# Feed-forward and projections in four 128-row column tiles instead of eight 64-row tiles, beside attention that stays in 64-row tiles

## The chip, the cores and the metric

One core of a Trainium2 chip runs the kernel. The metric is device time in microseconds (us); the median of two runs before the change is 1071.32 us (1070.79 to 1071.85). A change of 2% is 21.4 us.

The core has a matrix engine (TensorE, in the profile PE, with its weight loads as PEld), a vector engine (DVE), a scalar engine (ACT), a general engine (POOL) and queues that issue transfers (SP above all). Matmul results go to PSUM, a memory of 128 partitions that DVE and ACT read.

## The reference

```python
x = A_x                                            # 1 x 2048 x 512, float32
g = _sigmoid((x * gate_w).sum(-1, keepdims=True))
# attention: 32 query heads of 16 columns, one shared key and value head
q = (x @ wq).reshape(B, S, H, Dh).transpose(0, 2, 1, 3); k = x @ wk; v = x @ wv
p = softmax(einsum("bhqd,bkd->bhqk", q, k) * Dh ** -0.5)
a = einsum("bhqk,bkd->bhqd", p, v) ... reshape(B, S, H * Dh) @ wo
b = silu(x @ w1) @ w2                              # 512 -> 1792 -> 512
return g * a + (1 - g) * b
```

## The kernel before

All operands of the large products are split into two float16 parts, and a product of two such operands is three matmuls (high by high, high by low, low by high). The product of low by low is left out.

**Prologue** (`first_pass`, up to about 34 us): x comes in by transfers of 256 rows (`loads`, L305), is transposed on PE (`transposed`, L317) and split into `xs`; keys and values are made (`K`, L387), and the first two blocks of queries (`Q`, L125 to L127).

**Attention and feed-forward** (`attention`, the rest) are interleaved by hand on PE. There are 512 steps: 4 chunks of 512 queries, 4 groups of heads, 2 halves of a group, 16 tiles of 128 keys. The loop at L1082 takes two steps at a time; call one trip a *pair*. There are 256 pairs. A pair's order of work on PE is a string with one letter for each piece:

- `S` (`scores`, L1012): eight matmuls of 50 rows (contraction) by 32 columns, one for each of two row halves and four column strips of the array, 512 long. ACT then takes the exponential of 128 x 1024 (L1015). Four `S` a pair.
- `P` and `N` (`pv`, L1058): eight matmuls of 64 rows by 32 columns. A step is either one float32 product (`N`) or three short ones (`P`): upper half of the probabilities by `VH` and by `VL`, and the rest of them, which DVE has computed (`low`, L1036), by `VH`.
- `F`: one *slot* of the stream of other products: feed-forward up (`ffn_h`) and down (`ffn_o`), query blocks (`q_block`) and output projection (`out_proj`). Six slots a pair, in two *bursts* of three, and twelve (two bursts of six) where the pair is widened.

The two usual strings are `SFFFSFFFSPPPSBN` and `SFFFSFFFSNBSN`; the widened ones have `FFFFFF` for `FFF`. The first pair has its own, with `E` for products on the whole 128 by 128 array (`whole`, L766).

An output of the stream is a 128 x 512 block in one PSUM bank (`pM`, two banks). It has 12 products of 128 rows (6 in the last feed-forward group), and each goes to the array as matmuls of 32 columns (`Out.product`, L762). The stream (`stream`) works on two outputs at a time. In a slot a product of the *new* output goes to the upper 64 rows of the array (`lo`, four column strips) and a product of the *current* output to the lower 64 rows (`hi_`). So an output is visited twice, once for each half of the contraction, and its evacuation (`evict`) comes after the second visit. `drain` is called between the two visits at the very end alone (`ending`).

Late in the run (at 778 us), `gather` (L643) collects the largest values that were met, writes 128 numbers to DRAM (`md`, L649), reads them back as a row (L654) and sets a flag, by which a second pass of the whole would run with other scales. It does not run here.

Of the kernel before, what the change touches and what calls it, by code (L numbers as in the profile page):

```python
# [6 lines left out]
F32 = mybir.dt.float32  # L7
# [38 lines left out]
def kernel(  # L46
# [21 lines left out]
    nc = tc.nc  # L68
    _, S, D = x.shape
    F = w1.shape[1]  # L70
    DH = wk.shape[1]
    KD = D // 128
# [4 lines left out]
    x = x.rearrange("b s d -> (b s) d")  # L77
# [16 lines left out]
    ident = consts.tile([128, 128], F32)  # L94
# [110 lines left out]
    def identity(cst):  # L205
        jp = cst.tile([128, 128], F32)
        nc.gpsimd.iota(jp, pattern=[[1, 128]], base=0, channel_multiplier=-1, allow_small_or_imprecise_dtypes=True)
        nc.vector.tensor_scalar(ident, jp, 0.0, None, op0=OP.is_equal)
# [81 lines left out]
    def loads(sb, q_cols):  # L290

        wkr = sb.tile([128, KD, DH], F32)
        nc.scalar.dma_start(wkr, by_row(wk))
        wvr = sb.tile([128, KD, DH], F32)
        nc.scalar.dma_start(wvr, by_row(wv))
        gwr = sb.tile([128, KD], F32)
        nc.scalar.dma_start(gwr, gate_w.rearrange("(p k) -> p k", k=KD))
        xn = []
        wqr = sb.tile([128, KD, q_cols], F32)
        for c in range(NCH):  # L300
            t_ = sb.tile([128, 4, D], F32, name=f"xn{c}")
            if c == NCH - 1:
                nc.sync.dma_start(wqr, by_row(wq)[:, :, :q_cols])
            for a in range(2):
                nc.sync.dma_start(t_[:, 2 * a:2 * a + 2], x[c * 512 + a * 256:c * 512 + a * 256 + 256].rearrange("(t p) d -> p t d", p=128))  # L305
            xn.append(t_)
        wkv = sb.tile([128, KD, 64], F32)
        nc.gpsimd.memset(wkv, 0.0)
        nc.gpsimd.tensor_copy(wkv[:, :, 0:16], wkr)
        nc.gpsimd.tensor_copy(wkv[:, :, 32:48], wvr)  # L310
        nc.gpsimd.tensor_copy(flat(wkv[:, :, 48:49]), gwr)
        return xn, wqr, wkv
# [44 lines left out]
    def first_pass():  # L357
        with ExitStack() as pro:
            sb = pro.enter_context(tc.tile_pool(name="pro", bufs=1))
            wk_ = pro.enter_context(tc.tile_pool(name="prow", bufs=2))  # L360
            ps = pro.enter_context(tc.tile_pool(name="props", bufs=1, space=PSUM))
            identity(sb)
            nc.gpsimd.memset(mxs, 0.0)
            sel_k, selA, selB, m_one, hmask, m_k = masks(sb)
            xn, wqr, wkv = loads(sb, 256)
# [262 lines left out]
    def chores():  # L628

        todo = []  # L630
        for kt in range(KD):
            for h in range(2):
                todo.append(lambda kt=kt, h=h: absmax(mxs[:, M_X + 2 * kt + h:M_X + 2 * kt + h + 1], xs[:, 0, kt, h * S // 2:(h + 1) * S // 2]))
                todo.append(lambda kt=kt, h=h: absmax(mxs[:, M_1 + 2 * kt + h:M_1 + 2 * kt + h + 1], w1s[:, 0, kt, h * F // 2:(h + 1) * F // 2]))
        for f in range(0, FT_ALL, 2):
            todo.append(lambda f=f: absmax(mxs[:, M_2 + f // 2:M_2 + f // 2 + 1], flat(w2s[:, 0, f:f + 2])))
        for o in range(0, NO, 2):
            todo.append(lambda o=o: absmax(mxs[:, M_O + o // 2:M_O + o // 2 + 1], flat(wo_s[:, 0, o:o + 2])))

        todo.append(lambda: absmax(mxs[:, M_Q:M_Q + 1], flat(wqs[:, 0])))  # L640
        todo.append(lambda: absmax(mxs[:, M_VV:M_VV + 1], VF[:, :, 0:16], AX.XY))

        def gather():  # L643
            mt, mr = raw_[0][:, 0:32], raw_[0][:, 32:33]
            nc.vector.tensor_reduce(mr[0:64], um, axis=AX.X, op=OP.min)
            nc.vector.tensor_scalar(mxs[0:64, M_B:M_B + 1], mr[0:64], -1.0, SHIFT * LAM / ONE, op0=OP.mult, op1=OP.add)
            nc.vector.transpose(mt, mxs)
            nc.vector.tensor_reduce(mr, mt, axis=AX.X, op=OP.max)
            nc.sync.dma_start(md.rearrange("(p o) -> p o", o=1), mr)  # L649

        m, m1 = raw_[1][0:1, 0:128], raw_[1][0:1, 128:160]

        def row():
            nc.sync.dma_start(m, md.rearrange("(o p) -> o p", o=1))  # L654

        g = raw_[2][0:1, 0:4 * len(RANGES)].rearrange("p (a b) -> p a b", a=4)

        def check(n0):
            if n0 == 0:
                nc.vector.tensor_reduce(m1, m.rearrange("p (a b) -> p b a", a=4), axis=AX.X, op=OP.max)  # L660
            for n in range(n0, min(n0 + 3, len(RANGES))):
                a, b, lo, hi = RANGES[n]
                nc.vector.tensor_reduce(g[:, 0, n:n + 1], m1[:, a:b], axis=AX.X, op=OP.max)
                nc.vector.tensor_scalar(g[:, 1, n:n + 1], g[:, 0, n:n + 1], lo, None, op0=OP.is_lt)
                nc.vector.tensor_scalar(g[:, 2, n:n + 1], g[:, 0, n:n + 1], hi, None, op0=OP.is_gt)

        def verdict():
            nc.vector.tensor_tensor(g[:, 3], g[:, 1], g[:, 2], op=OP.max)
            nc.vector.tensor_reduce(g[:, 0, 0:1], g[:, 3], axis=AX.X, op=OP.max)
            nc.vector.tensor_copy(flag, g[:, 0, 0:1])  # L670

        return todo, gather, row, *(lambda n=n: check(n) for n in range(0, len(RANGES), 3)), verdict


# [47 lines left out]
    def attention(ctx, scale_of, t_scale, shifts, split_pieces, chores, q_todo, bounds, early, gates_):  # L722
# [187 lines left out]
            return o  # L910

        seq, ahead, ended, debt = outs(), [], [None], [18]
        drains, left = [0], [4 * len(blocks)]
        turn = [None, 0]
        lo, hi_ = slice(0, 64), slice(64, 128)
        plain, ending = [False], [False]

        def stream():

            cur = None  # L920
            while True:
                if plain[0] and cur is None:
                    return
                new = None if plain[0] else follow()
                n_new = len(new.mm) if new else 0
                n_cur = len(cur.mm) if cur else 0
                n = -(-max(n_new, n_cur) // 6) * 6


                if cur and drains[0] == cur.count and ending[0]:  # L930
                    drain()
                for i in range(n):
                    turn[:] = cur, n - i - 1
                    for m in range(4):
                        if i < n_new:
                            new.product(i, lo, m, i == 0, False)
                        if i < n_cur:
                            cur.product(i, hi_, m, False, i == n_cur - 1)
                    if i < n - 1:
                        yield False  # L940
                if cur:
                    cur.evict(cur.bank)
                    ended[0] = cur
                cur = new
                if cur:
                    cur.count = drains[0]
                yield True

        def drain():

            nc.tensor.drain()
            drains[0] += 1

        def norm_a(pv, rb, st):

# [125 lines left out]
        prefetch(0)  # L1081
        for s in range(0, len(steps) + 2, 2):  # L1082
            on = s < len(steps)
            ending[0] = not on
            if on and steps[s][1] == 0:
                i = steps[s][0]
                prefetch(i + 1)
                if q_todo and i % 2 == 0:
                    queue.append(q_todo.pop(0))
            p, more = 2 * s, True  # L1090
            slots, order = SPLIT, [(s - 2, 0), (s - 2, 1), (s - 2, 2), (s - 1, 3)]
            if s - 2 in native:
                slots, order = NATIVE, [(s - 2, 3), (s - 1, 3)]
            if not s and early:
                slots = FIRST
            wide[0] = debt[0] >= 6 and ended[0] is not None and ended[0].hidden
            if wide[0]:
                slots = WIDE[slots]
            ended[0], n_f, bounded[0] = None, 0, False
            for a in slots:  # L1100
                if a == "S" and on:
                    scores(p)
                    p += 1
                elif a == "E":
                    next(whole_, None)
                elif a == "F" and more:
                    more = not next(work)
                    n_f += 1
                elif a == "B" and (bound_now() or s == 4 and bounds):
                    bound()  # L1110
                    bounded[0] = True
                    while lq and lq[0][0] <= p - 3:
                        low(*lq.pop(0))
                elif a in "PN" and s >= 2:
                    pv(*order.pop(0))
            debt[0] -= max(n_f - 6, 0)
            if gates_ and s == 4:
                gates_()
                spend(0.6)
            fill(4.95 if n_f > 6 else 4.1 if ended[0] and ended[0].hidden else 3.7)  # L1120
# [65 lines left out]
```

## Time and profile before

| what | value |
|---|---|
| median of the runs | 1071.32 us |
| the profiled execution | 1071.37 us, its span 1069.5 us |
| granted TensorE clock | 0.998 |
| PE busy | 1047.9 us, 31236 matmuls |
| PEld busy | 662.3 us, 31236 weight loads |
| ACT busy | 1006.2 us, 1116 instructions |
| DVE busy | 769.8 us, 1064 instructions |
| POOL busy | 24.2 us, 54 instructions |

The span is from the first to the last instruction. Busy time is the union of an engine's instructions; matmuls overlap one another, so the start of one and the start of the next tell more than a duration does. A shape such as 64*32 in the profile is the rows by columns of the array that a matmul uses.

### The profile page before, as it was taken

Reading aid. Unit: us, or ns where it says so; the run is one execution under the profiler, and the core shown is the slowest. Engines: PE = TensorE matmul, PEld = TensorE weight load, DVE = VectorE, ACT = ScalarE, POOL = GpSimd, SP = SyncE. Lnnn points to the kernel's source line nnn. Section 1 sums busy time; section 2 is a strip of 40 time slices with the busy share of each in tenths; the row PEclk is TensorE's granted clock in tenths of the full one; section 3 lists DMA queues with packets and bytes.
Section 4 is the critical chain, followed back from the end, with each engine's and each line's share of the span. In section 5 each row is a group of like instructions: output and inputs, shape, how many; then the busy total and the mean of one; then the engine's idle time right before and its main releaser. Section 6 shows DMA issues by size and latency. Waiting matters only on the chain.

```text
span 1069.5 us, 65974 instructions
## 1 busy us (share of the span) xinstructions
PE 1047.9 (98%) x31236; PEld 662.3 (62%) x31236; DVE 769.8 (72%) x1064; ACT 1006.2 (94%) x1116; POOL 24.2 (2%) x54
## 2 busy tenths in 40 slices
PE   7999999999999999999999999999999999999996
PEld 5456766667566577766655567686756565555552
DVE  6676776677778686978776696775857767475875
ACT  5899999999999999999999999899989999999993
POOL 1110010100000000000000000000000000000000
PEclk9999999999999999999999999999999999999999
DMA  6321111210001000000000100000000010000001
GB/s 219 108 66 43 44 47 45 61 41 21 6 11 50 22 22 12 14 12 21 12 11 21 39 27 12 22 12 12 22 4 11 31 32 12 12 7 8 12 4 44
DMA packets 20840, 32.95 MB, mean 31 GB/s; under 512 B 5137, under 2 KB 12050, under 8 KB 20562
## 3 DMA queue, kind: packets, MB, share of 16 engines
q1 hardware_dynamic: 17618, 20.46, 6.0%
q0 software_dynamic: 2512, 8.13, 2.6%
q8 instruction: 246, 4.03, 1.6%
q14 instruction: 32, 0.26, 0.1%
q10 hardware_dynamic: 432, 0.07, 0.0%
HBM read 20.12 MB, written 8.52 MB: 27 GB/s over the span
## 4 chain that ended last, share of the span: by engine, by line
PE 90%; ACT 4%; DVE 3%; issue 2%; DMA 1%; SPq 0%; POOL 0%; DVEq 0%; POOLq 0%; ACTq 0%
PE pv L1058 36%; PE pm L762 32%; PE S L1012 20%; ACT P L1015 4%; PE pt L317 1%; DVE acc L743 0%; DMA xn<-in_A_x_dram 0%; DVE T L958 0%; PE pk L387 0%; DVE U L959 0%; DMA raw<-in_B_w_dram 0%; DVE T L960 0%; DVE C L965 0%; DMA qd<-qs__367 0%; DMA qb<-qd 0%
## 5 line engine op out<-in xcount | busy, mean ns | idle before, releaser
L1015 ACT ACTIVATE P<-S 128x1024 f32<-128x1024 f32 x1024 | 964.0, 1050 | 24.7 <-PE S L1012 15.9
L1012 PE MATMUL S<-qb,KT 50*32 50x512 f16 x8192 | 478.1, 378 | 2.7 <-issue 1.4
L1036 DVE TENSOR_TENSOR L<-P 128x1024 f16<-128x1024 f32 x332 | 389.4, 1217 | 7.1 <-ACT P L1015 7.1
L1058 PE MATMUL pv<-P,VF 64*32 64x512 f32 x5536 | 383.1, 589 | 0.4 <-issue 0.4
L1012 PEld LDWEIGHTS <-KT 50*32 50x32 f16 x8192 | 188.8, 90 | 193.7 <-issue 124.7
L762 PE MATMUL pm<-w2s,H 64*32 64x512 f16 x5328 | 261.4, 375 | 0.6 <-issue 0.2
L762 PE MATMUL pm<-xs,w1s 64*32 64x512 f16 x5376 | 249.3, 375 | 1.3 <-DVE acc L743 0.6
L762 PEld LDWEIGHTS <-H 64*32 64x32 f16 x5328 | 144.6, 93 | 45.8 <-issue 12.7
L762 PEld LDWEIGHTS <-w1s 64*32 64x32 f16 x5376 | 136.2, 93 | 43.8 <-issue 12.5
L1058 PEld LDWEIGHTS pv<-P,VF 64*32 64x32 f32 x5536 | 127.4, 107 | 32.1 <-issue 10.1
L811 DVE SCALAR_TENSOR_TENSOR e<-e,pm 128x512 f32<-128x512 f32 x56 | 38.4, 686 | 141.4 <-ACT e L810 141.3
L762 PE MATMUL pm<-xs,wqs 64*32 64x512 f16 x1152 | 79.7, 375 | 0.0
L1058 PE MATMUL pv<-P,VH 64*32 64x512 bf16 x1328 | 77.6, 389 | 0.0
L1058 PE MATMUL pv<-P,VL 64*32 64x512 bf16 x1328 | 77.2, 385 | 0.0
L1058 PE MATMUL pv<-L,VH 64*32 64x512 f16 x1328 | 76.2, 374 | 0.0
L1058 PEld LDWEIGHTS <-VH 64*32 64x32 f16 x2656 | 56.9, 92 | 18.2 <-issue 2.3
L762 PE MATMUL pm<-wo_s,O 64*32 64x512 f16 x1440 | 64.3, 375 | 0.0
L743 DVE SCALAR_TENSOR_TENSOR acc<-pm,g,acc 128x512 f32<-128x512 f32 x47 | 35.0, 745 | 31.5 <-PE pm L762 31.5
L958 DVE STREAM_TRANSPOSE T<-pv 128x512 f32<-128x512 f32 x32 | 22.9, 717 | 48.1 <-PE pv L1058 36.9
L762 PEld LDWEIGHTS <-wqs 64*32 64x32 f16 x1152 | 41.8, 93 | 11.7 <-issue 3.6
L762 PEld LDWEIGHTS <-O 64*32 64x32 f16 x1440 | 30.0, 93 | 17.2 <-issue 2.6
L810 ACT ACTIVATE e<-pm 128x512 f32<-128x512 f32 x56 | 34.4, 615 | 6.4 <-PE pm L762 6.4
(159 smaller groups left out, 463.4 us busy)
## 6 DMA issues: line engine op xcount, KB each, us to landing
qb<-qd SPq DMA_DIRECT2D x192, 32.0 KB
raw<-in_B_w_dram POOLq DMA_DIRECT2D x23, 256.0 KB, 3.1
xn<-in_A_x_dram SPq DMA_DIRECT2D x8, 512.0 KB
out_dram<-acc SPq DMA_DIRECT2D x16, 256.0 KB
qd<-qx SPq DMA_DIRECT2D x12, 256.0 KB
raw<-in_A_wo_dram POOLq DMA_DIRECT2D x4, 256.0 KB, 2.9
qb<-sh SPq DMA_DIRECT2D x62, 2.0 KB
raw<-in_B_w_dram SPq DMA_DIRECT2D x3, 256.0 KB
```

Of the source, the lines that this page charges most:

```text
L317: nc.tensor.transpose(pt[:, kt], xn[c].rearrange("p t (d k) -> p t k d", k=KD)[:, t, kt], ident)
L743: nc.vector.scalar_tensor_tensor(a, po, gate[:, n:n + 1], a, op0=OP.mult, op1=OP.add)
L762: nc.tensor.matmul(self.bank[32 * m:32 * m + 32], l(i, rows, 32 * m), r(j, rows), start=first, stop=last)
L810: nc.scalar.activation(e, ph, AF.Tanh, scale=t_scale)
L811: nc.vector.scalar_tensor_tensor(e, e, 1.0, ph, op0=OP.add, op1=OP.mult)
L958: nc.vector.transpose(T, pv[0])
L1012: nc.tensor.matmul(sc[32 * m:32 * m + 32, f], KT[b:b + 50, k0:k0 + 32], qtile[i][b:b + 50, j], start=True, stop=True)
L1015: nc.scalar.activation(P[:, 2 * j:2 * j + 2], sc, AF.Exp, scale=scale_of(c, o))
L1036: nc.vector.tensor_tensor(lows[s][:, q], P[:, q], upper(P)[:, q], op=OP.subtract)
L1058: nc.tensor.matmul(pvs[i][h][32 * j:32 * j + 32], a[r], b[r, j], start=first, stop=last)
```

## The change

The stream's products are put on the array as four tiles of 128 rows by 32 columns, all for one output. A slot is then four matmuls over the full contraction, and an output is visited once. Scores and P V stay as they were. `drain` and the code around it go. Three smaller edits come with it: 15 transposes of the identity at the start, whose result nobody reads; the first 256 rows of x in two transfers of 128; and in `gather` one more 32 by 32 block transpose on DVE, so that the 128 numbers leave as four rows of 32 instead of 128 single ones.

```diff
@@ loads
-            for a in range(2):
-                nc.sync.dma_start(t_[:, 2 * a:2 * a + 2], x[c * 512 + a * 256:c * 512 + a * 256 + 256].rearrange("(t p) d -> p t d", p=128))
+            for a, b in ((0, 1), (1, 2), (2, 4)) if c == 0 else ((0, 2), (2, 4)):
+                nc.sync.dma_start(t_[:, a:b], x[c * 512 + a * 128:c * 512 + b * 128].rearrange("(t p) d -> p t d", p=128))
@@ first_pass
             identity(sb)
+            pt = ps.tile([128, KD, 128], F32, name="pt", bufs=4)
+            for _ in range(15):
+                nc.tensor.transpose(pt[:, 0], ident, ident)
@@ gather
-            mt, mr = raw_[0][:, 0:32], raw_[0][:, 32:33]
+            mt, mr, mq = raw_[0][:, 0:32], raw_[0][:, 32:33], raw_[0][:, 64:96]
...
-            nc.sync.dma_start(md.rearrange("(p o) -> p o", o=1), mr)
+            nc.vector.transpose(mq, raw_[0][:, 32:64])
+            nc.sync.dma_start(md.rearrange("(a b) -> a b", a=4), mq[0:128:32])
@@ stream
-            cur = None
             while True:
-                if plain[0] and cur is None:
+                if plain[0]:
                     return
-                new = None if plain[0] else follow()
-                n_new = len(new.mm) if new else 0
-                n_cur = len(cur.mm) if cur else 0
-                n = -(-max(n_new, n_cur) // 6) * 6
-                if cur and drains[0] == cur.count and ending[0]:
-                    drain()
-                for i in range(n):
-                    turn[:] = cur, n - i - 1
-                    for m in range(4):
-                        if i < n_new:
-                            new.product(i, lo, m, i == 0, False)
-                        if i < n_cur:
-                            cur.product(i, hi_, m, False, i == n_cur - 1)
-                    if i < n - 1:
+                o = follow()
+                if o is None:
+                    yield True
+                    continue
+                n = len(o.mm)
+                for i in range(-(-n // 6) * 6):
+                    turn[:] = o, -(-n // 6) * 6 - i - 1
+                    if i < n:
+                        for m in range(4):
+                            o.product(i, slice(0, 128), m, i == 0, i == n - 1)
+                    if i < -(-n // 6) * 6 - 1:
                         yield False
-                if cur:
-                    cur.evict(cur.bank)
-                    ended[0] = cur
-                cur = new
-                if cur:
-                    cur.count = drains[0]
+                o.evict(o.bank)
+                ended[0] = o
                 yield True
```

The order of PE's instructions at the end of a burst, before. L762 is a product of the stream, L1012 the scores; `pm` is an output's bank, `H` the feed-forward's inner values, `KT` the keys.

```order
L762 LDWEIGHTS w1s_67
L762 MATMUL pm_5667<-xs_66,w1s_67 32x512
L762 LDWEIGHTS H_1737
L762 MATMUL pm_5382<-w2s_68,H_1737 32x512
L1012 LDWEIGHTS KT_60
L1012 MATMUL S_5692<-qb1_84,KT_60 32x512
```

Two outputs (`pm_5667` and `pm_5382`) take turns, each on its 64 rows, and the scores follow in tiles of the same size. The same place with the change (L768 is then the stream, L1003 the scores):

```order
L768 LDWEIGHTS H_753
L768 MATMUL pm_2577<-w2s_68,H_753 32x512
L1003 LDWEIGHTS KT_60
L1003 MATMUL S_2590<-qb0_83,KT_60 32x512
L1003 LDWEIGHTS KT_60
L1003 MATMUL S_2590<-qb0_83,KT_60 32x512
```

One output alone fills the slot, with 128 rows a matmul, and then the tiles change to 64 rows. The whole program of the first pass has 13,296 stream matmuls in tiles of 64 rows before and 6,672 in tiles of 128 rows with the change; they stand in 508 bursts before and in 502 with the change.

On DVE, `gather` before (L645 to L648; L811 and L1036 are the feed-forward's activation and `low`):

```order
L645 TENSOR_REDUCE raw0_80<-um_75 64x1
L646 TENSOR_SCALAR mxs_78<-raw0_80 64x1
L647 STREAM_TRANSPOSE raw0_80<-mxs_78 128x32
L648 TENSOR_REDUCE raw0_80<-raw0_80 128x1
L811 SCALAR_TENSOR_TENSOR e_24624<-e_24624,pm_24141 128x512
```

and with the change, one transpose longer:

```order
L650 TENSOR_REDUCE raw0_80<-um_75 64x1
L651 TENSOR_SCALAR mxs_78<-raw0_80 64x1
L652 STREAM_TRANSPOSE raw0_80<-mxs_78 128x32
L653 TENSOR_REDUCE raw0_80<-raw0_80 128x1
L654 STREAM_TRANSPOSE raw0_80<-raw0_80 128x32
L817 SCALAR_TENSOR_TENSOR e_19362<-e_19362,pm_19192 128x512
```

The transfer of `md` that SP issues behind it changes from 128x1 to 4x32 elements.

More of the change, by code (lines that the diff above doesn't have):

```diff
@@ L912, in attention @@
         seq, ahead, ended, debt = outs(), [], [None], [18]
-        drains, left = [0], [4 * len(blocks)]
+        left = [4 * len(blocks)]
         turn = [None, 0]
         lo, hi_ = slice(0, 64), slice(64, 128)
-        plain, ending = [False], [False]
+        plain = [False]
         def stream():
-            cur = None
             while True:
-                if plain[0] and cur is None:
+                if plain[0]:
                     return
-                new = None if plain[0] else follow()
-                n_new = len(new.mm) if new else 0
-                n_cur = len(cur.mm) if cur else 0
-                n = -(-max(n_new, n_cur) // 6) * 6
-                if cur and drains[0] == cur.count and ending[0]:
-                    drain()
-                for i in range(n):
-                    turn[:] = cur, n - i - 1
-                    for m in range(4):
-                        if i < n_new:
-                            new.product(i, lo, m, i == 0, False)
-                        if i < n_cur:
-                            cur.product(i, hi_, m, False, i == n_cur - 1)
-                    if i < n - 1:
-                        yield False
-                if cur:
-                    cur.evict(cur.bank)
-                    ended[0] = cur
-                cur = new
-                if cur:
-                    cur.count = drains[0]
+                o = follow()
[9 more added lines that the diff above has]
+                    if i < -(-n // 6) * 6 - 1:
+                        yield False
+                o.evict(o.bank)
+                ended[0] = o
                 yield True
-        def drain():
-            nc.tensor.drain()
-            drains[0] += 1
         def norm_a(pv, rb, st):
@@ L1083, in attention @@
             on = s < len(steps)
-            ending[0] = not on
             if on and steps[s][1] == 0:
```

## The prediction

> **What bounds the kernel now.** I read the page's busy times first, then its chain of waits.
>
> ```profile
> PE 1047.9 (98%) x31236; PEld 662.3 (62%) x31236; DVE 769.8 (72%) x1064; ACT 1006.2 (94%) x1116; POOL 24.2 (2%) x54
> ...
> PE 90%; ACT 4%; DVE 3%; issue 2%; DMA 1%; SPq 0%; POOL 0%; DVEq 0%; POOLq 0%; ACTq 0%
> ```
>
> PE is busy 98% of the span and makes 90% of the chain that ends last, so PE's time counts one for one. ACT is close behind. How close, one pair shows; this is PE's timeline (start, length, engine, line, operation, shape, count).
>
> ```profile
> 1002.50 0.41 PE L1012 MATMUL S<-qb,KT 50*32 50x512 f16 x8
> 1002.72 0.84 PE L762 MATMUL pm<-w2s,H 64*32 64x512 f16 x24
> 1003.37 0.41 PE L1012 MATMUL S<-qb,KT 50*32 50x512 f16 x8
> 1003.59 0.84 PE L762 MATMUL pm<-w2s,H 64*32 64x512 f16 x24
> 1004.23 0.41 PE L1012 MATMUL S<-qb,KT 50*32 50x512 f16 x8
> 1004.45 0.42 PE L1058 MATMUL pv<-P,VH 64*32 64x512 bf16 x8
> 1004.68 0.42 PE L1058 MATMUL pv<-P,VL 64*32 64x512 bf16 x8
> 1004.91 0.41 PE L1058 MATMUL pv<-L,VH 64*32 64x512 f16 x8
> 1005.12 0.41 PE L1012 MATMUL S<-qb,KT 50*32 50x512 f16 x8
> 1005.34 1.05 PE L1058 MATMUL pv<-P,VF 64*32 64x512 f32 x16
> 1006.20 0.41 PE L1012 MATMUL S<-qb,KT 50*32 50x512 f16 x8
> ```
>
> Eight matmuls of 64 by 32 start together and the next eight start 0.217 us later: a *pass*. A burst is three passes (1003.59 to 1004.23), the float32 product four (1005.34 to 1006.20). The pair is 4 + 6 + 3 + 4 = 17 passes, 3.68 us at 0.2165, and it took 3.70. ACT's four exponentials take as long:
>
> ```profile
> 999.33 1.69 ACT P L1015 x2
> 1002.06 2.67 ACT P L1015 x3
> 1005.70 2.73 ACT P L1015 x3
> ```
>
> From the chain: whatever waits for ACT recurs every 3.70 us, 0.925 an exponential. PE and ACT are balanced to 0.02 us here. So **nothing that PE gains in such a pair is worth more than 0.02 us, and everything it loses is paid in full.**
>
> Scores follow a burst without a seam now (0.65 from 1003.59 to 1004.23 for three passes), since all tiles have 64 rows.
>
> **The change part by part.**
>
> *Passes.* A slot streams 512 columns either way. Now eight tiles take one pass; with the change four tiles of 128 by 32 do. That four run at once is not shown, but two tiles of 128 by 64 are (first row):
>
> ```profile
> 24.06 2.78 PE L387 MATMUL pk<-xs,wkvs 128*64 128x512 f16 x24
> 26.77 0.39 PE L125 MATMUL pq<-xs,wqs 128*128 128x512 f16 x1
> ```
>
> 12 passes of two in 26.77 - 24.06 = 2.71 us, 0.226 each with a change of tiles at the end. So halving the matmuls and weight loads halves nothing: a slot stays 0.2165. Counting the program's order, the stream goes from 1689 passes (some half filled, where an output of 12 products meets one of 6) to 1668, the three-part P V steps from 166 to 171 (+15 passes) and the float32 ones from 346 to 341 (-20): 26 passes fewer, **-5.6 us**.
>
> *Changes of tile size.* Each burst now begins and ends with one: 502 bursts, 1004 changes. The first pair of the kernel before has the like, between scores and products on the whole array:
>
> ```profile
> 34.80 0.41 PE L1012 MATMUL S<-qb,KT 50*32 50x512 f16 x8
> 35.14 1.04 PE L766 MATMUL pm<-xs,wqs 128*128 128x512 f16 x4
> 36.10 0.41 PE L1012 MATMUL S<-qb,KT 50*32 50x512 f16 x8
> 36.45 1.04 PE L766 MATMUL pm<-xs,wqs 128*128 128x512 f16 x4
> 37.41 0.41 PE L1012 MATMUL S<-qb,KT 50*32 50x512 f16 x8
> 37.76 1.04 PE L766 MATMUL pm<-xs,wqs 128*128 128x512 f16 x4
> 38.73 0.41 PE L1012 MATMUL S<-qb,KT 50*32 50x512 f16 x8
> ```
>
> From 34.80 to 38.73 are 15 passes, 3.25 us without seams; they took 3.93. Six changes cost 0.68, 0.114 each. There rows and columns both change. A change of rows alone (16 rows to 128, all columns) is 30.21 to 30.53 here:
>
> ```profile
> 29.36 0.38 PE L127 MATMUL pq<-xs,wqs 128*128 128x512 f16 x1
> 29.67 0.39 PE L348 MATMUL pk<-qa,kab 64*32 64x512 f16 x2
> 29.99 0.39 PE L327 MATMUL pt<-k,selA 16*128 16x512 f16 x2
> 30.21 0.38 PE L328 MATMUL pt<-k,selB 16*128 16x512 f16 x2
> 30.53 0.66 PE L416 MATMUL pt<-ident,vr 128*128 128x128 f32 x4
> ```
>
> 0.32 instead of 0.22 (selA to selB, same tiles), so 0.10 as well; and 0.31 and 0.32 on the two rows above it. Every change of tile in the trace costs 0.09 to 0.12. 64 by 32 to 128 by 32 is not in it. Its bounds are nothing (same column strips) and, as a full stop, the record's 0.38 less the pass's 0.217 plus a weight load of 0.093:
>
> ```profile
> L762 PEld LDWEIGHTS <-H 64*32 64x32 f16 x5328 | 144.6, 93 | 45.8 <-issue 12.7
> ```
>
> 0.26. I take 0.12, near the first pair's row, a little more since the stretch of 24.06 to 26.77 loses 0.11 over one exit and a slow first pass: 1004 x 0.12 = **+120.5 us**. What queues behind the change is the scores, then ACT, which has 0.44 us to spare in a pair of 4.15.
>
> The Trainium skill says in TensorEngine Tiling (Array Packing), Tiling Modes, that going to another tiling mode, though not to another tile, drains TensorE. By TensorE: Matmul & The Clock Gate, Single matmul latency, a lone warm matmul of 512 columns takes (398 + 512)/2.4 = 379 ns, against a gap of 216, so a drain would be an estimated 0.163 us and this term +164; the trace agrees on the seam, and shows 0.114 for its size.
>
> *Given back.* Where PE now waits for ACT, PE's longer pair swallows the wait. The passes before sum to 4595 x 0.2165 = 995 us (1024 scores, 498 and 1384 of P V, 1689 of the stream), plus 3 for the whole products from 33.92 on; the stretch from there to the last burst (start 1054.01, 1.3 long) is 1021. So at most some 22 us are to be had. The start, the end and the gather keep half of that: **-8 us** (bounds 0 and -17).
>
> *Gather.* 128 packets of one number hold something up; the waits of SP's queue and of the engines, and PE's timeline, have:
>
> ```profile
> SPq L654 <- DMA md<-raw: 7.8, 1, 7.8
> ```
>
> ```profile
> ACT P L1015 <- remote: 3.0, 1, 3.0
> ```
>
> ```profile
> 784.78 0.39 PE L1012 MATMUL S<-qb,KT 50*32 50x512 f16 x3 [1.40 <-issue]
> ...
> 786.39 0.59 PE L1058 MATMUL pv<-P,VF 64*32 64x512 f32 x1 [0.36 <-issue]
> ```
>
> The write of `md` took 7.8 us from its issue at 778.7, and inside that window PE and ACT both stood still, waiting for nothing that the profile names. I read it as instruction loads held up by the small packets. Four packets should end it: **-2.7 us** (0 to -4); the added DVE transpose costs 0.2 in a wait of DVE.
>
> *Prologue.* The first transposes run slowly (a stretch, its length, PE's busy time and instructions, granted clock, share of the transfer engines, GB/s):
>
> ```profile
> 4.97:9.28 4.31, 4.31 (x21) 1.00 1.05 384
> 9.28:10.80 1.52, 1.52 (x13) 1.00 1.05 388
> ```
>
> 0.205 us each for 4.3 us, then 0.117, while the granted clock reads 1.00 in both. Fifteen more ahead of the first transfer would move the break forward. x arrives at 384 GB/s, 1.4 us for 8 transposes, so 0.17 each is the floor: 20 x 0.04 plus 0.4 for the earlier first transfer, **-1.2 us** (0 to -2.2).
>
> *End.* The bursts at 1050.78 and 1054.01 are gone, as one visit ends an output earlier: **-1.5 us** (0 to -3).
>
> ```profile
> 1050.78 1.49 PE L762 MATMUL pm<-w2s,H 64*32 64x512 f16 x48 [0.16 <-DVE L L1036]
> ```
>
> The evacuation moves up to the end of the only visit; the other bank is free for the next output's 12 slots, two pairs, so its 0.6 on ACT and 0.7 on DVE stay covered. `qd` writes move up by one group of loads on SP, which waits there anyway.
>
> **Sum:** 120.5 - 5.6 - 8 - 2.7 - 1.2 - 1.5 = +101.5 on the profiled execution's 1071.4, which is the median to 0.1: **1173 us**.
>
> **Rivals.**
>
> *The change of rows is free where the column strips stay.* For it: the bound above, and that each strip's weights are loaded by themselves. Against: 30.21 to 30.53, where only rows changed. It leaves -5.6, of which ACT's 3.70 lets some 3 through, and the small terms: 1071 - 3 - 5 = **1063**, within 2%. It decides below about 0.04 us a change, where 1004 of them and the savings come to 21 us. Chance 0.09.
>
> *A full stop.* 0.26 a change: 1071 + 261 - 19 = **1313**. Against: six of six seams at 0.114, whose records are as long (0.38). Chance 0.04.
>
> *Weights no longer load ahead.* Tiles of 128 rows leave no other rows free; 1668 slots would each pay 0.093: 1173 + 155 = **1328**. Against: the stretch from 24.06, where both tiles use all rows and a pass stays near 0.2165. Chance 0.03.
>
> The Trainium skill states this last as a rule (TensorE: Matmul & The Clock Gate, Part 3, What overlaps and what doesn't): a weight load overlaps matmuls in flight only if its row group differs. By that rule the time would be that rival's; the trace does not bear it out, with 12 passes in 2.71 us.
>
> **How the numbers follow.** My forecast has 0.82, for 1130 (each change 0.092, 20 us given back) to 1200 (0.135 a change, nothing given back). With the rivals' 0.16 and 0.02 between, the range of 1125 to 1200 leaves out under 2 in 10. About 2% (21 us) is what this kernel's measurement can tell from no change: faster 0.02, same 0.09, slower 0.89.
>
> **What would show it.** In the new profile's timeline, scores to burst and burst to scores 0.31 to 0.34 us apart instead of 0.22; a usual pair 4.1 to 4.2 us; ACT's busy share down to some 86%; PE's matmuls down by 6,600; no stop of PE and ACT after `md`. Pairs of 3.70 would prove me wrong at the seam; slots above 0.22 inside a burst, at the weights.

## The result, and the profile after

The changed kernel takes 1175.96 us (1174.87 to 1177.06) against 1071.32: 1.0978 times as long, interval 1.0961 to 1.0996. The forecast was 1173. The profiled execution's span is 1174.8 us, 105.3 more than before.

Busy times, from the page of the changed kernel:

```profile
PE 1155.1 (98%) x24661; PEld 420.2 (36%) x24661; DVE 781.6 (67%) x1075; ACT 1061.8 (90%) x1116; POOL 23.9 (2%) x54
```

PE has 6,575 matmuls fewer and is busy 107 us longer. The pair that answers to the one quoted above, from PE's timeline:

```profile
1104.08 0.40 PE L1003 MATMUL S<-qb,KT 50*32 50x512 f16 x8
1104.41 0.83 PE L768 MATMUL pm<-w2s,H 128*32 128x512 f16 x12
1105.18 0.41 PE L1003 MATMUL S<-qb,KT 50*32 50x512 f16 x8
1105.52 0.83 PE L768 MATMUL pm<-w2s,H 128*32 128x512 f16 x12
1106.28 0.41 PE L1003 MATMUL S<-qb,KT 50*32 50x512 f16 x8
1106.50 0.41 PE L1049 MATMUL pv<-P,VH 64*32 64x512 bf16 x8
1106.73 0.41 PE L1049 MATMUL pv<-P,VL 64*32 64x512 bf16 x8
1106.96 0.40 PE L1049 MATMUL pv<-L,VH 64*32 64x512 f16 x8
1107.18 0.40 PE L1003 MATMUL S<-qb,KT 50*32 50x512 f16 x8
1107.39 1.04 PE L1049 MATMUL pv<-P,VF 64*32 64x512 f32 x16
1108.26 0.40 PE L1003 MATMUL S<-qb,KT 50*32 50x512 f16 x8
```

The pair takes 4.18 us instead of 3.70. From scores to burst are 0.33 to 0.34 us instead of 0.22, from the burst's start to the next scores 0.76 to 0.77 instead of 0.64 or 0.65, and everything that stays in 64-row tiles is as it was (1106.28 to 1108.26). Over the bursts of three slots between two scores passes (some 440), the median from scores to scores is 1.100 us; for those of the kernel before (some 420) it is 0.868. So a burst costs **0.232 us** more, 0.120 on the way in and 0.112 on the way out. Within a burst, by medians, the second slot starts 0.226 after the first (0.219 before), the third 0.216 after the second (0.215), the scores 0.319 after the third (0.215), and the four column tiles of a slot begin within 0.010: they do run together. 502 bursts x 0.232 = 116.5 us.

### The profile page after: what moved, and what is told of

Same layout as the page of the kernel before. It is cut to its first block, busy times and chain, and to the rows that moved or that the text cites. A ratio compares the mean times of both kernels' runs of the same rounds, so it can differ in the third digit from the quotient of the medians.

```text
span 1174.8 us, 52835 instructions
## 1 busy us (share of the span) xinstructions
PE 1155.1 (98%) x24661; PEld 420.2 (36%) x24661; DVE 781.6 (67%) x1075; ACT 1061.8 (90%) x1116; POOL 23.9 (2%) x54
## 5 line engine op out<-in xcount | busy, mean ns | idle before, releaser
L1006 ACT ACTIVATE P<-S 128x1024 f32<-128x1024 f32 x1024 | 1018.6, 1025 | 72.2 <-PE S L1003 29.5
L1003 PE MATMUL S<-qb,KT 50*32 50x512 f16 x8192 | 421.5, 382 | 2.0 <-ACT P L1006 1.8
L1003 PEld LDWEIGHTS <-KT 50*32 50x32 f16 x8192 | 134.5, 89 | 343.4 <-issue 320.0
L768 PE MATMUL pm<-w2s,H 128*32 128x512 f16 x2688 | 183.9, 382 | 0.0
L768 PE MATMUL pm<-xs,w1s 128*32 128x512 f16 x2688 | 178.5, 382 | 0.6 <-DVE qx L880 0.6
L768 PEld LDWEIGHTS <-w1s 128*32 128x32 f16 x2688 | 55.0, 95 | 105.9 <-issue 72.4
L768 PEld LDWEIGHTS <-H 128*32 128x32 f16 x2688 | 52.0, 95 | 112.7 <-issue 85.6
L768 PE MATMUL pm<-wo_s,O 128*32 128x512 f16 x720 | 49.8, 383 | 0.0
L121 DVE TENSOR_TENSOR H<-e,H 128x512 f16<-128x512 f32 x56 | 38.8, 692 | 1.9
L768 PE MATMUL pm<-xs,wqs 128*32 128x512 f16 x576 | 39.9, 383 | 0.0
L749 DVE SCALAR_TENSOR_TENSOR acc<-pm,gg,acc 128x512 f32<-128x512 f32 x18 | 13.4, 747 | 19.2 <-PE pm L768 15.7
```

What stands on the lines that cost most here:

```text
L121: nc.vector.tensor_tensor(a2, a, a1, op=OP.subtract)
L749: nc.vector.scalar_tensor_tensor(a, po, gate[:, n:n + 1], a, op0=OP.mult, op1=OP.add)
L768: nc.tensor.matmul(self.bank[32 * m:32 * m + 32], l(i, rows, 32 * m), r(j, rows), start=first, stop=last)
L1003: nc.tensor.matmul(sc[32 * m:32 * m + 32, f], KT[b:b + 50, k0:k0 + 32], qtile[i][b:b + 50, j], start=True, stop=True)
L1006: nc.scalar.activation(P[:, 2 * j:2 * j + 2], sc, AF.Exp, scale=scale_of(c, o))
```

## The experiments

### Fewer seams, same work

```diff
-SPLIT, NATIVE = "SFFFSFFFSPPPSBN", "SFFFSFFFSNBSN"
+SPLIT, NATIVE = "SFFFFFFSSPPPSBN", "SFFFFFFSSNBSN"
-WIDE = {SPLIT: "SFFFFFFSFFFFFFSPPPBSN", NATIVE: "SFFFFFFSFFFFFFSNBSN"}
+WIDE = {SPLIT: "SFFFFFFFFFFFFSSPPPBSN", NATIVE: "SFFFFFFFFFFFFSSNBSN"}
```

On the changed kernel:

> The changed kernel with a pair's two bursts put together (SFFFFFFSSPPPSBN and SFFFFFFSSNBSN, twelve slots in one where widened): the same matmuls, about 255 bursts instead of 502. Theory (each change of tile size costs PE 0.116 us, wherever it stands): 247 bursts x 0.232 = 57 us fewer, 1176 - 57 = 1119 us, and at most 15 more where scores that stand together wait for ACT. Rival (the 128-row tiles themselves are slower, slot by slot, through weights or banks): no fewer slots, so 1170 to 1180.

On the kernel before, as its control:

> Control: the kernel before with the same merged strings. It has no changes of tile size to save. Theory: 1071 to 1085 us, what the new order costs through waits for ACT; e1 less this gives the price of the seams that are left, 255 x 0.232 = 59 us. Rival (slots are slower): the difference to e1 stays at 105.

Both expectations missed: 1218.74 us (1.1366 times the kernel before, 1.1347 to 1.1385) and 1170.71 (1.0927, 1.0908 to 1.0945). The control's waits tell why (engine, what waited for what, us, times, longest):

```profile
ACT P L1015 <- PE S L1012: 85.9, 200, 1.9
PE S L1012 <- ACT P L1015: 59.2, 208, 0.5
```

Two scores passes side by side starve ACT during the long burst, and then PE waits for ACT; before, the first of these was 15.9. The order costs 99 us without any change of tile, more than the 57 that it could save. The difference of the two, 48 us for 253 bursts, is what the seams cost there, 0.19 each before the other savings of the change are added back (they are in the part on why the prediction was right).

A second try, with two scores passes ahead of the burst so that ACT has work in hand (widened pairs unchanged):

```diff
-SPLIT, NATIVE = "SFFFSFFFSPPPSBN", "SFFFSFFFSNBSN"
+SPLIT, NATIVE = "SSFFFFFFSPPPSBN", "SSFFFFFFSNBSN"
```

> The changed kernel with the usual pairs' two bursts put together, and two scores passes ahead of the burst (SSFFFFFFSPPPSBN, SSFFFFFFSNBSN), so that ACT has two exponentials in hand while the burst runs; widened pairs as they were. 280 bursts instead of 502, the same matmuls. Theory (0.232 a burst, and the order that was tried before lost its gain to waits for ACT): 222 x 0.232 = 51.5 us fewer, 1176 - 51 = 1125 us, up to 10 more for waits that are left. Rival (PE pays for the stream's matmuls, not for the seams): 1170 or more.

> The kernel before with the order SSFFFFFFSPPPSBN and SSFFFFFFSNBSN: control to the changed kernel in the same order, which took 1193.7 us in 280 bursts although it has 222 fewer than before the reordering. There ACT waited 0.44 us a pair for the third scores pass behind the long burst, and PE for ACT. Theory (the seams are paid here too, now on a path through ACT: 280 x 0.232 = 65): about 1130. Rival (the reordering made the seams free and all of the loss is the order): 1190.

1193.68 us (1.1139, 1.1122 to 1.1156), missed again, and 1136.66 for the control (1.0607, 1.0591 to 1.0623), near what was then expected of it. One scores pass, the burst and the next scores, of the changed kernel in this order:

```profile
601.22 0.41 PE L1003 MATMUL S<-qb,KT 50*32 50x512 f16 x8 [0.16 <-ACT P L1006]
601.56 1.48 PE L768 MATMUL pm<-w2s,H 128*32 128x512 f16 x24
602.97 0.41 PE L1003 MATMUL S<-qb,KT 50*32 50x512 f16 x8
```

and of the control:

```profile
701.17 0.41 PE L1012 MATMUL S<-qb,KT 50*32 50x512 f16 x8
701.38 1.49 PE L762 MATMUL pm<-xs,w1s 64*32 64x512 f16 x48
702.68 0.41 PE L1012 MATMUL S<-qb,KT 50*32 50x512 f16 x8
```

1.75 against 1.51 us: the seams are 0.24 here as well. But the pair is now paced by a ring of PE and ACT (a scores pass waits for the exponential that frees its bank, 0.16 us above; the exponential waits for the scores behind the burst, 0.44 at 603.51), and the long burst lies on it. That this ring makes all of the loss is argued and not shown. The difference of the two is 57 us for 280 bursts.

### More seams, nearly the same work

```diff
-SPLIT, NATIVE = "SFFFSFFFSPPPSBN", "SFFFSFFFSNBSN"
+SPLIT, NATIVE = "SFFSFFSFFPPPSBN", "SFFSFFSFFNBSN"
```

> The changed kernel with three bursts of two slots in a usual pair instead of two of three (SFFSFFSFFPPPSBN, SFFSFFSFFNBSN): 728 bursts instead of 502, the same matmuls, scores no further apart than now. PE sets the pace here, so no wait for ACT should blur the price. Theory: 226 x 0.232 = +52, 1176 + 52 = 1228 us. Rival (the price is for the slots or for the stream's matmuls as such): 1176.

1231.28 us (1.1485, 1.1467 to 1.1503): +55.3 over the changed kernel for 226 more bursts. The work is not quite the same, though it was expected to be: the page has 24541 matmuls instead of 24661, because 15 steps of P V are one float32 product instead of three short ones. These are 15 passes more, 3.2 us, which leaves 52.1 us or **0.230** for each burst. PE's waits for ACT come to 1.5 us in the whole run and blur nothing. It settles that the price goes with the edges of the bursts and not with their slots:

```profile
700.49 0.42 PE L1003 MATMUL S<-qb,KT 50*32 50x512 f16 x8
700.84 0.61 PE L768 MATMUL pm<-xs,wqs 128*32 128x512 f16 x8
701.38 0.41 PE L1003 MATMUL S<-qb,KT 50*32 50x512 f16 x8
701.72 0.61 PE L768 MATMUL pm<-xs,wqs 128*32 128x512 f16 x8
702.27 0.41 PE L1003 MATMUL S<-qb,KT 50*32 50x512 f16 x8
```

### Which part of the tile's form changes

Columns alone, on the kernel before: each half-contraction as one matmul of 64 rows by 128 columns (`half`, its definition left out here).

```diff
-                    for m in range(4):
-                        if i < n_new:
-                            new.product(i, lo, m, i == 0, False)
...
+                    if i < n_new:
+                        new.half(i, lo, i == 0, False)
+                    if i < n_cur:
+                        cur.half(i, hi_, False, i == n_cur - 1)
```

> The kernel before, two outputs at a time on 64 rows each, but each product as one matmul of 64 rows by 128 columns instead of four of 32 columns: at the burst's edges columns change and rows stay. Theory (any change of the tile's form costs the same): 508 bursts x 0.232 = 118 less what is given back, 1170 to 1185 us. Rival (only a change of rows costs): 1071. Second rival (what costs is the number of matmuls or weight loads in a burst): 6 instead of 24, so 1071 or less.

Rows and columns both, on the changed kernel:

```diff
-                        for m in range(4):
-                            o.product(i, slice(0, 128), m, i == 0, i == n - 1)
+                        o.whole(i, i == 0, i == n - 1)
```

> The changed kernel with each slot as one matmul on the whole 128 by 128 array instead of four column tiles. Theory: rows and columns change at the same 1004 places, 0.114 each as in the first pair: 1174 to 1178 us. Rival (the four column tiles do not quite run together, or their weights are late): faster than 1165. Rival (a change of both rows and columns costs twice): 1290.

1173.04 us (1.0946, 1.0928 to 1.0964) and 1172.08 (1.0944, 1.0926 to 1.0962). The first lies in the range that was expected, the second 2 us below it. Columns alone, rows alone (the change itself) and both cost nearly the same: 0.34 us into a burst in all three, and 0.225, 0.232 and 0.225 for a burst of three slots by the medians. The 0.007 lie on the way out (0.309 us from the last slot to the scores instead of 0.319); why is not shown. Here columns alone, then both:

```profile
503.22 0.41 PE L1015 MATMUL S<-qb,KT 50*32 50x512 f16 x8
503.56 0.39 PE L766 MATMUL pm<-xs,w1s 64*128 64x512 f16 x1
503.57 0.39 PE L766 MATMUL pm<-w2s,H 64*128 64x512 f16 x1
```

```profile
502.61 0.41 PE L1002 MATMUL S<-qb,KT 50*32 50x512 f16 x8
502.95 0.82 PE L772 MATMUL pm<-xs,w1s 128*128 128x512 f16 x3
```

The number of matmuls plays no part: a slot is 8, 4, 2 or 1 of them in these kernels. The kernel before is fast because scores, P V and stream share *one* form of tile.

### A stop in place of a change

On the kernel before, at each edge of a burst:

```diff
                 elif a == "F" and more:
+                    if was != "F":
+                        nc.tensor.drain()
...
+                if was == "F" and a != "F":
+                    nc.tensor.drain()
```

> The kernel before, all tiles of 64 rows, with a PE drain instruction at each edge of a burst, 1016 in all: a plain stop where the changed kernel changes its tiles. Theory A (a change of tiles is such a stop, no more): 0.116 each, 1170 to 1185 us. Theory B (a change of tiles keeps the next instructions flowing and only the array runs empty, while a drain instruction also holds up the queue and the weight loads): 0.2 us each or more, 1270 and up. Rival (stops at these places are hidden): 1071.

1406.01 us (1.3117, 1.3097 to 1.3137): 334 us for 1016 drains, 0.33 each.

```profile
704.30 0.84 PE L762 MATMUL pm<-w2s,H 64*32 64x512 f16 x24
705.26 0.41 PE L1012 MATMUL S<-qb,KT 50*32 50x512 f16 x8
705.80 0.84 PE L762 MATMUL pm<-w2s,H 64*32 64x512 f16 x24
```

From scores to burst are 0.54 us. So the change of tiles is cheaper than a drain instruction by a factor of nearly three. At a change of tiles the next tile starts 0.309 us after the last start of the old one (medians of the changed kernel, the same in both directions), before that matmul's record (0.38) ends. What the hardware does in those 0.1 us these runs don't show. The Trainium skill (TensorEngine Tiling (Array Packing), Tiling Modes) calls it a drain of TensorE on a change of mode: that only a change of mode costs, and every change that was tried, agrees with all runs here. The prediction's estimate of 0.163 from the lone matmul's latency is 0.05 too high.

### The small edits alone, on the kernel before

The gather's transpose and four-row write:

> The kernel before with the change's edit of the gather alone (one more DVE transpose, 4 rows of 32 to DRAM). Theory: the write lands in 2 us instead of 8, PE and ACT no longer stand still behind it, 2.5 to 3.5 us less: 1068. Rival (the stop behind the write was an accident of instruction loads): 1071, and a stop of the same kind elsewhere or in the same place.

1067.84 us, 0.9965 (0.9951 to 0.9978): **4 us less, the fastest kernel of the study**. The wait of SP's queue for the write is 1.0 us instead of 7.8, and neither PE nor ACT stops behind it:

```profile
SPq L655 <- DMA md<-raw: 1.0, 1, 1.0
```

The 15 transposes:

> The kernel before with the 15 transposes of the identity at the start alone. Theory: the transposes of x run at 0.12 us from the first or from the second group on, but x itself arrives at 0.17 us for each, so the first scores pass (33.9 us before) starts 0.5 to 1 us earlier. Rival (the first transposes' speed hides behind the arrival of x): no change in the start of the scores.

1071.96 us, 0.9999 (0.9989 to 1.0008), not resolved. Yet they do what they should. From PE's timeline:

```profile
1.38 3.20 PE L365 MATMUL pt<-ident 128*128 128x128 f32 x15 [1.38 <-DVE ident L208]
4.88 1.23 PE L317 MATMUL pt<-ident,xn 128*128 128x128 f32 x8 [0.30 <-DMA xn<-in_A_x_dram]
6.37 1.23 PE L317 MATMUL pt<-ident,xn 128*128 128x128 f32 x8 [0.26 <-DMA xn<-in_A_x_dram]
```

Eight transposes take 1.23 us instead of 1.71 and then wait for x; the scores start at 33.12 instead of 33.92. That is 0.07% of the time, less than the interval's width. The trace also shows where it was lost again. Behind the gather PE stands for 2.47 us at a time (1.40 in the kernel before), and from 785.8 us on the granted clock is 0.50 for 3.4 us (a stretch, with the busy times of PE, PEld, DVE, ACT and POOL, then the clock):

```profile
785.80:789.20 3.40, 3.40 (x56) 2.35 (x61) 0.00 (x0) 2.01 (x2) 0.00 (x0) 0.50 0.00 0
```

Half the clock for 3.4 us is an estimated 1.7 us. The trace of the kernel before has no such stretch there. Of the eleven runs, three have a mean clock of 0.998 and spans of 1068.0 to 1069.4 us, the eight others 0.996 or 0.997 and 1069.2 to 1070.8. So the transposes seem to save something near a microsecond, and the half clock to take it back; the two were not tried apart.

The first transfer in two:

> The kernel before with the first 256 rows of x in two transfers alone. In the changed kernel x came in more slowly between 4 and 7 us and PE waited 1.3 us for the second group. Theory: the one more transfer in the queue does that, and the first scores pass starts 0.5 us later here too, 34.4 us. Rival (it was an accident of that execution): the first transposes start up to 0.5 us earlier and the scores at 33.9 or a little earlier.

1072.40 us, 1.0007 (0.9998 to 1.0016), not resolved; the trace shows a loss at the start:

```profile
4.07 4.05 PE L317 MATMUL pt<-ident,xn 128*128 128x128 f32 x16 [4.07 <-DMA xn<-in_A_x_dram]
9.08 1.31 PE L317 MATMUL pt<-ident,xn 128*128 128x128 f32 x5 [0.95 <-DMA xn<-in_A_x_dram]
```

The first transposes begin 0.9 us earlier, then x is late by 0.95, the transposes are still slow at 9.08 (0.21 each), and the scores start at 35.37, later than the 34.4 expected. Not all of this is the split's. The traces hold records of the granted clock, and the views count time without a record as 1.00. In this run the first record, at full clock, begins at 13.4 us, in the kernel before at 9.5; in both the transposes take 0.213 us each up to that point and 0.120 after it. Transfers of the whole core move 282 GB/s from 4.8 to 8 us, against 385 before; the changed kernel has 294.

### The end, with PE kept busy

On the changed kernel, ahead of the last output projection:

```diff
+        for _ in range(18):
+            nc.tensor.matmul(banks[0], w2s[:, 0, 0, 0:128], xs[:, 0, 0, 0:512], start=True, stop=True)
```

> The changed kernel with 18 more products on the whole array (3.9 us, nobody reads them) between the last P V product and the last output projection, where PE now stands still for 3.9 us. Theory (the stand lets the granted clock fall to 0.5, and the 12 products after it take 0.427 us instead of 0.216): they run at 0.216 again, 12 x 0.21 = 2.5 us less, 1173.5, and 1.00 in the clock of the last stretch. Rival (the clock falls for another reason): 1176.

1174.23 us, 1.0961 (1.0946 to 1.0975), 1.7 us less than the changed kernel; the intervals overlap, but from the last scores to the span's end are 17.9 us instead of 20.4. The changed kernel's timeline:

```profile
1161.10 1.03 PE L772 MATMUL pm<-wo_s,O 128*128 128x512 f16 x2 [3.85 <-DVE O L120]
1161.93 1.06 PE L772 MATMUL S<-wo_s,O 128*128 128x512 f16 x2
```

and a stretch of it, with the granted clock, 0.50:

```profile
1163.00:1166.00 3.00, 3.00 (x8) 0.91 (x6) 0.84 (x2) 0.00 (x0) 0.00 (x0) 0.50 0.02 5
```

The same with the filler:

```profile
1160.41 0.60 PE L772 MATMUL pm<-wo_s,O 128*128 128x512 f16 x2
1160.86 0.59 PE L772 MATMUL S<-wo_s,O 128*128 128x512 f16 x2
```

```profile
1160.00:1163.00 3.00, 3.00 (x15) 1.15 (x13) 1.48 (x3) 0.00 (x0) 0.00 (x0) 1.00 0.00 0
```

0.427 us a product becomes 0.216. The Trainium skill says of this (TensorE: Matmul & The Clock Gate, HAM oscillation) that idle gaps of PE beyond some 3.4 us drop its clock to half; the trace agrees, 0.50 after 3.85 us, and 1.00 before the change, where the longest stand at the end was 1.35. How much such a stand costs varies: with the whole products (a stand of 3.86 us) the first five of the last 12 still ran at full clock, and with the second merged order (3.86 too) the last four. Nor does it take a stand of that length: with the 15 transposes alone, 0.50 followed at the gather on a longest stand of 2.47.

## Why the prediction was right, point by point

| step | forecast, us | shown |
|---|---|---|
| changes of tile | +120.5 (0.120 each) | +116.5 (0.116 each, both traces) |
| passes | -5.6 (26 passes) | -3.0 (14 passes up to the last scores; counted, not timed apart) |
| gather | -2.7 | -4.0 (interval -5.3 to -2.4), tried alone |
| prologue | -1.2 | +0.5 in the two traces: scores start at 34.45 instead of 33.92 |
| end | -1.5 | +0.3 from the last scores to the span's end, 12 passes fewer included |
| given back | -8 | -5.0, what is left of 105.3 |
| sum | +101.5 | +105.3 in the span |

The mechanism was right. That the sum came within 4 us is in part luck, since the small terms' errors have both signs: changes of tile and gather came out 5.3 us lower than forecast, the other four 9.1 higher.

**The price and its place** held: what the first pair showed for scores beside whole products held for every form of tile, and the bound of nothing for a change of rows alone was wrong as the row at 30.21 said. The price of 0.116 is far from the nothing and the 0.26 of the first two rivals. Three pairs of kernels with the same order give nearly the same price. From the first to the last scores, the traces of a pair differ by 104.5, 47.4 and 56.7 us. With 7.0 us for the 14 passes and the gather added back, that is 0.222, 0.215 and 0.228 for each of 502, 253 and 280 bursts; the waits given back are still in these figures. For the merged orders this leans on the gather's saving being the same there, which was not tried.

**Passes and end** overlap in the forecast. Of the 26 passes, 12 are the bursts at 1050.78 and 1054.01, behind the last scores: six of them are most of the 1.5 us forecast for the end, and the other six ran while DVE normalised, where PE had time to spare.

**Weights ahead**: the rival is out, with 0.216 from second to third slot. The first slot's 0.226 is above the 0.22 named as its sign, but only 0.007 above the kernel before, where the rival needs 0.093; and a whole product in place of four column tiles gives 0.226 as well.

**Given back**: its reason held better than its size. Between 100 and 1000 us, the gather left out, the usual intervals from scores to scores are together some 7 us longer in the kernel before than the same passes need in the changed one; so PE's waits lay all along the run, and most of these went. Why only 5.0 are left in the balance stays open.

**ACT's margin** rested on a weak reading. The 0.925 for an exponential is the pair's own 3.70 over four. Exponentials that overlap the one before them start 0.902 to 0.920 us apart in the trace, so four need 3.61 to 3.68, and the margin was between 0.02 and 0.09 us. That a loss of PE is paid in full doesn't hang on it.

**The prologue** failed as a step, and two traces can't give its size. I priced both edits by the arrival of x as it was, and the split changed that arrival: all transfers together move 282 to 303 GB/s between 4.8 and 8 us in the seven kernels with the split. In the six traces with the changed prologue the scores start between 33.68 and 36.27 us, in the six with the old one between 33.74 and 34.21; no gain shows. I also took the 1.00 of the view for a full clock. In all 14 traces the transposes (but for the first of a group) take 0.213 us before the first clock record and 0.120 after it. That the clock was at half before is not recorded, but in one trace (the first merged order on the changed kernel) it fell back for 3.4 us, and there the 0.213 returns:

```profile
8.90:12.40 3.50, 3.50 (x17) 3.50 (x18) 1.61 (x3) 2.05 (x4) 3.09 (x7) 0.51 1.06 392
```

**The end** failed in its cover: the bursts at 1050.78 and 1054.01 went, and the last P V matmul starts 2.28 us after the last scores instead of 3.82, as forecast. But they, with the whole products behind them, had kept PE's clock up while DVE normalised; that cost 1.9 us behind the last P V matmul, more than the 1.5 gained.

**ACT's share** was forecast at 86% and is 90%. Its exponentials no longer overlap one another (by 0.115 us in the median before), so their union counts more time; it has the spare time all the same.

## What to carry to other kernels

Where short stretches of small matmuls alternate on TensorE, give them the same tile form, even at the price of more instructions and of two outputs in flight: here one form costs nothing at the border, another one 0.112 to 0.116 us each time, whether rows, columns or both differ. Before merging stretches to save borders, look at who needs the alternation; here ACT's next exponential did, and the saving turned into a loss of 65 to 99 us. And before removing the last work of an engine, ask whether it keeps the clock up for what follows.

## What was not expected of the hardware

- A write of 128 packets of 4 bytes took 7.8 us to land and went with a stop of ACT of 3.0 us and of PE of 1.8 (1.40 and 0.36); as 4 packets it took 1.0 us with no stop. In the seven traces with 128 packets it took 7.2 to 8.5 us and PE stood in six, up to 4.1 us at a time; with 64 by 128 tiles (7.7 us) neither engine stopped. So the slow write doesn't always bring the stop, and that instruction loads were held up in between is argued and not shown.
- A drain instruction on PE cost 0.33 us in a full stream, a change of tile 0.116.
- Float32 transposes at the start took 0.213 us each up to a trace's first record of the granted clock, at 4.2 to 13.4 us, and 0.120 after it.
- One transfer of 512 KB as two of 256 KB lowered what all transfers moved between 4.8 and 8 us: 282 to 303 GB/s in the seven traces with the split, 381 to 389 in six without it and 321 in the one with drains. Why stays open.
